# One decode step of attention and SwiGLU side by side: the products with V moved into the pass that scores the same group

## The chip, the core and the metric

The kernel runs on one core of one Trainium2 chip. Its time is the device time of one execution in microseconds; each figure is the median of several runs of the same program. The core has TensorE (PE in the profile, with PEld for its weight loads), VectorE (DVE), ScalarE (ACT), GpSimd (POOL) and SyncE (SP), and sixteen DMA engines that all queues share.

## What is computed

One token of four sequences goes through a layer norm, and then through two branches whose results are added to the input: attention over the last 4096 positions of a cache, and a SwiGLU feed-forward block.

```python
# B = 4 sequences, 1 token each, D = 512; Hq = 32 query heads, Hkv = 8, Dh = 128, W = 4096, F = 1792
xn = layernorm(x)
q = xn @ wq                                   # 32 heads of 128
k, v = k_cache[:, :, Sk - W:], v_cache[:, :, Sk - W:]     # each head of the cache serves 4 query heads
p = softmax(q k^T * Dh ** -0.5)
A = (p v).reshape(B, 1, Hq * Dh) @ wo
Bf = (silu(xn @ w_gate) * (xn @ w_up)) @ w_down
out = x + A + Bf
```

All inputs are bf16. What is read comes to 81 MB: 32 MiB each of K and V, 4 MiB each of wq and wo, and 1.75 MiB each of the three feed-forward matrices.

## The kernel before, in words

**Tiling.** The cache is worked off by head ("group"), eight of them. Position and sequence lie across the 128 partitions: a partition holds 128 consecutive positions of one sequence, so that a group's K is a tile of 128 partitions x 128 positions x 128 values (`KB`, 4 MiB), and V the same (`VB`). The scores of all 16 pairs of sequence and query head are computed for every position, and those of other sequences are masked out by a large negative shift. TensorE transposes K in chunks of eight positions (16 chunks, `transposes`, line 424) into three PSUM banks `ps_kt`; DVE (line 341) or, for five of the chunks, ACT (line 293) copies each to SBUF as `KT`; `scores` (line 437) multiplies it by the queries into one of four PSUM banks `ps_S`, 32 positions each. DVE takes maxima bank by bank (line 345). When all are there, `maxima` (line 444) transposes them, DVE forms the correction `CM` (lines 350 to 354), and `shift` (line 449) adds it to the four banks. ACT exponentiates each bank into `P` (line 297).

**Lag.** The products with V are one group behind. In pass r TensorE scores K of group r and, behind the shift, multiplies P of group r - 1 by V of group r - 1 (`pv`, line 460, 128 matmuls of 32 rows each, four column groups); pass 0 does this with zeros, for which POOL clears P and `VB` (lines 241 and 242). ACT's exponentials of pass r wait until `pv` of the same pass has read the old P (line 294, semaphore s_pv). The denominators are eight matmuls with ones ahead of `pv` (`dens`, line 468). DVE's `norm` (lines 356 to 368) sums the denominators (line 358), copies the product out of PSUM (line 360), waits for TensorE's `fin` (lines 476 and 477), which adds up the four parts, and writes the normalised result to `OT`. The spins (line 481) are matmuls whose result nobody reads.

**The order of the work** is written out by hand on each engine; nothing is scheduled. On TensorE a pass is: 16 chunks of transposes and scores, spins, `maxima`, spins, `shift`, `dens`, `pv`, three spins, `fin`. On DVE: copies and maxima, correction, and then `norm` of the previous group. The loop runs eight times. Behind it, outside the loop, stand `pv` and `dens` of the last group (lines 523 and 524), W_down (`down`, line 499), `fin` and `norm` of the last group, a permutation (line 531), and the products with W_o (lines 535 to 546): the first 22 of its 32 row tiles in one PSUM bank with four row groups, which ACT copies out (line 305), the other ten straight into the result, as the pieces of W_o land.

**Transfers.** SP's queue issues all the large ones, in one order (lines 261 to 275): wq, w_gate, w_up, K0 in two halves, then (when the projection is done, s_q) V7 into the buffer that held wq (`VL`), six row tiles of W_o, and then for each g from 1 to 7 the two halves of K(g) and V(g - 1); at the end W_down and the rest of W_o in four pieces. There is one buffer for K and one for V. A half of K is issued when the transposes of that half of the previous group are done (line 251), V when `pv` has read the V before (line 255). A wait on SP holds up everything that stands behind it.

Of the kernel before, what the change touches and what calls it, by code (L numbers as in the profile page):

```python
# [3 lines left out]
BF16 = mybir.dt.bfloat16  # L4
FP32 = mybir.dt.float32
# [5 lines left out]
def bass_parallel_sum__sliding_block_cached__swiglu_ffn__decode_kernel(  # L11
# [34 lines left out]
    OFF = -1.0e9  # L46
    WOS = (0, 6, 22, 27, 30, 32)
    WOE = 22
# [66 lines left out]
    O_ps = ps_O[:, 0:Dh]  # L115
    OL_ps = ps_kt[0][:, 0:Dh]
# [20 lines left out]
    d_out = sem("d_out")  # L137
    d_wo = [sem("d_wo%d" % q) for q in range(5)]
    d_k = [sem("d_k%d" % s) for s in range(2)]
    d_v = sem("d_v")  # L140
    d_vl = sem("d_vl")
    s_const = sem("s_const")
# [19 lines left out]
    s_pv = sem("s_pv")  # L162
    s_dp = sem("s_dp")
    s_oc = sem("s_oc")
    s_dn = sem("s_dn")
# [21 lines left out]
    with nc.Block() as block:  # L187

        @block.gpsimd
        def _(eng):  # L190
# [50 lines left out]
            eng.memset(P[:], 0.0)  # L241
            eng.memset(VB[:].rearrange("p t d -> p (t d)").bitcast(FP32), 0.0)  # L242
            eng.drain().then_inc(s_zero, 1)

        @block.sync
        def _(eng):
            H = NT // 2

            def load_k(g, h):
                if g > 0:  # L250
                    eng.wait_ge(s_tr, NCH * (g - 1) + (h + 1) * NCH // 2)
                eng.dma_start(KB[:, h * H:(h + 1) * H, :], kv_ap(A_k_cache, g, h * H, (h + 1) * H)).then_inc(d_k[h], 16)

            def load_v(g):
                eng.wait_ge(s_pv, g + 1)
                eng.dma_start(VB[:], kv_ap(A_v_cache, g, 0, NT)).then_inc(d_v, 16)  # L256
# [4 lines left out]
            eng.dma_start(WQ, wq_ap).then_inc(d_wq, 16)  # L261
# [12 lines left out]
            for q in range(1, 5):  # L274
                load_wo(q, WOS[q], WOS[q + 1])
            eng.wait_ge(s_y, 1)
            for n in range(2):
                eng.dma_start(out_ap[n], y[32 * n:32 * n + B, :]).then_inc(d_out, 16)
            eng.wait_ge(d_out, 64)

        @block.scalar
        def _(eng):
            eng.dma_start(X[:], x_ap).then_inc(d_x, 16)
            eng.wait_ge(s_var, 1)
            eng.activation(st_std[:], st_var[:], ACT.Sqrt).then_inc(s_std, 1)
            eng.wait_ge(s_const, 1)
            for n in range(4):
                eng.dma_start(X4[32 * n:32 * n + B, :], x4_ap[n]).then_inc(d_x4, 16)

            def group(r):  # L290
                for n, c in enumerate(ACT_CH):
                    eng.wait_ge(s_tr, r * NCH + (c + 1))
                    eng.activation(KT[:, c % 4], kt_ps[c % 3], ACT.Copy).then_inc(s_ea, 1)  # L293
                eng.wait_ge(s_pv, r + 1)
                for q in range(NB):
                    eng.wait_ge(s_mk, r * NB + (q + 1))
                    eng.activation(P[:, BT * q:BT * (q + 1), :], ps_S[q][:].rearrange("p (t n) -> p t n", n=NH),  # L297
                                   ACT.Exp, scale=SCALE).then_inc(s_p, 1)
# [12 lines left out]
        def _(eng):  # L311
# [24 lines left out]

            def group(r):
                for c in range(NCH):
                    if c not in ACT_CH:
                        eng.wait_ge(s_tr, r * NCH + (c + 1))  # L340
                        eng.tensor_copy(KT[:, c % 4], kt_ps[c % 3]).then_inc(s_ev, 1)  # L341
# [13 lines left out]

            def norm(r, O=O_ps):
                eng.wait_ge(s_dp, r + 2)
                eng.tensor_reduce(dsum[:], den_ps.rearrange("p (t n) -> p n t", n=NH), AX.X, ALU.add).then_inc(s_dn, 1)  # L358
                eng.wait_ge(s_pv, r + 2)
                eng.tensor_copy(Osb[:], O).then_inc(s_oc, 1)  # L360
                eng.wait_ge(s_fin, r + 2)
# [28 lines left out]
        def _(eng):  # L390
# [23 lines left out]
            eng.sem_inc(s_p, NB)  # L414
            eng.sem_inc(s_nrm, 2)
            eng.sem_inc(s_dn, 1)
            eng.sem_inc(s_oc, 1)
            eng.sem_inc(d_v, 16)

# [32 lines left out]

            def pv(r, V, O):
                for t in range(NT):
                    n = t % 4
                    if t % BT == 0:
                        eng.wait_ge(s_p, r * NB + (t // BT + 1))
                    if t % BT == BT - 1 and t < NT - 1:
                        eng.wait_ge(s_p, r * NB + (t // BT + 2))
                    last = mm(O[32 * n:32 * n + 32, :], P[:, t:t + 2, :].rearrange("p t n -> p (t n)"), V[:, t, :],  # L460
                              start=(t < 4), stop=(t >= NT - 4), skip_group_check=True)
                return last

            def dens(r):
                eng.wait_ge(s_p, r * NB + NB)
                for e in range(NT // DT):
                    n = e % 4
                    last = mm(den_ps[32 * n:32 * n + 32, :], ones[:, 0:32],  # L468
                              P[:, DT * e:DT * (e + 1), :].rearrange("p t n -> p (t n)"),
                              start=(e < 4), stop=(e >= NT // DT - 4), skip_group_check=True)  # L470
                return last

            def fin(r):
                eng.wait_ge(s_oc, r + 1)
                eng.wait_ge(s_dn, r + 1)
# [49 lines left out]
            down()  # L525
            eng.wait_ge(s_nrm, HKV + 1)
            fin(HKV)
            spin(2)
            eng.wait_ge(s_nrm, HKV + 2)
            for b in range(B):  # L530
# [3 lines left out]
            eng.wait_ge(s_pc, 1)  # L534
            for q in range(5):
                eng.wait_ge(d_wo[q], 16)
# [5 lines left out]
                if WOS[q + 1] == WOE:  # L542
                    last.then_inc(s_e, 1)
                if q == 2:
                    eng.wait_ge(s_ec, 1)
# [30 lines left out]
```

## Time and profile before

| | before |
|---|---|
| median of 3 runs | 198.21 us (197.14 to 198.66) |
| the profiled execution | 198.13 us |
| its span | 196.4 us |
| TensorE busy | 161.6 us (82% of the span) |
| DVE busy | 108.1 us (55%) |
| ACT busy | 61.0 us (31%) |
| POOL busy | 18.7 us (10%) |
| mean granted clock of TensorE | 0.972 |
| rate of the transfers over the span | 413 GB/s |

The span is the stretch that the profile covers; the 1.7 us around it are not in any row. A row of the timeline starts with its start and its length in microseconds, then engine, line, operation, output and inputs, and how many instructions it merges; in brackets stands how long the engine was idle before and what ended the idleness. The row of a window gives its stretch and length, then busy time and instructions of PE, PEld, DVE, ACT and POOL, the granted clock, the busy share of the DMA engines and GB/s. A row of transfers gives tile and source, queue, count, size of one, and the time from issue to landing; a landing is counted when all sixteen engines have delivered.

### The profile page before, as it was taken

What the parts mean: (1) busy time and instruction counts of PE and PEld (TensorE: products, weight loads), DVE (VectorE), ACT (ScalarE), POOL (GpSimd) and SP (SyncE); (2) the same over time, 40 slices, a digit from 0 to 9 for tenths busy, and PEclk for the clock granted to TensorE, in tenths of its full rate; (3) what the DMA queues carried; (4) which work ended last, traced back from release to release, by engine and by line L of the source; (5) the groups of instructions that cost most, each with busy time, mean ns of one, the idle gap of its engine ahead of it and who ended that gap; (6) DMA issues with size and microseconds to landing.
All of it is one profiled execution on the core that took longest, in us unless ns stands there. A gap on an engine that the chain in (4) does not pass through costs nothing.

```text
span 196.4 us, 8531 instructions
## 1 busy us (share of the span) xinstructions
PE 161.6 (82%) x3778; PEld 134.8 (69%) x3778; DVE 108.1 (55%) x217; ACT 61.0 (31%) x77; POOL 18.7 (10%) x52
## 2 busy tenths in 40 slices
PE   0137679938999979988998899799979999999983
PEld 0137679925996679568956895599459966994841
DVE  4205336841487268726872686268625882786240
ACT  2020004600562245233513451445042622550401
POOL 8879300000000000000000000000000000000000
PEclk9999999975999999999999999999996999999999
DMA  6999999989999999999999999999999999999991
GB/s 214 427 441 418 435 430 467 450 380 420 400 420 399 427 467 430 400 437 450 434 410 430 454 427 417 430 461 434 407 430 464 434 400 430 464 434 398 429 384 38
DMA packets 4833, 81.15 MB, mean 413 GB/s; under 512 B 596, under 2 KB 600, under 8 KB 1112
## 3 DMA queue, kind: packets, MB, share of 16 engines
q1 hardware_dynamic: 4768, 81.01, 96.8%
q8 instruction: 7, 0.11, 0.2%
q10 hardware_dynamic: 56, 0.01, 0.0%
q14 instruction: 2, 0.02, 0.0%
HBM read 81.01 MB, written 0.00 MB: 413 GB/s over the span
## 4 chain that ended last, share of the span: by engine, by line
DMA 63%; PE 30%; DVE 2%; SPq 2%; issue 2%; DVEq 0%
DMA kbuf<-in_A_k_cache_dram 50%; PE ps_kt L424 18%; DMA wo_sb<-in_A_wo_dram 13%; PE ps_s L437 5%; PE ps_o L460 2%; PE ps_kt L481 2%; PE ps_s L449 1%; DVE kT L341 1%; SPq L259 1%; PE ps_kt L468 0%; DVE mx L345 0%; SPq L273 0%; SPq L256 0%; PE ps_kt L444 0%; SPq L263 0%
## 5 line engine op out<-in xcount | busy, mean ns | idle before, releaser
L424 PE MATMUL ps_kt<-ident,kbuf 128*128 128x128 bf16 x1024 | 78.3, 224 | 8.7 <-DMA kbuf<-in_A_k_cache_dram 8.6
L341 DVE COPY kT<-ps_kt 128x1024 bf16<-128x1024 bf16 x88 | 57.8, 686 | 24.6 <-PE ps_kt L424 24.6
L424 PEld LDWEIGHTS ps_kt<-ident,kbuf 128*128 128x128 bf16 x1024 | 60.8, 100 | 9.4 <-DMA kbuf<-in_A_k_cache_dram 9.4
L293 ACT ACTIVATE kT<-ps_kt 128x1024 bf16<-128x1024 bf16 x40 | 40.9, 1023 | 41.3 <-PE ps_kt L424 41.3
L437 PE MATMUL ps_s<-qC,kT 128*128 128x16 bf16 x1024 | 44.9, 170 | 4.7 <-DVE kT L341 2.4
L437 PEld LDWEIGHTS ps_s<-qC,kT 128*128 128x128 bf16 x1024 | 37.2, 97 | 6.6 <-DVE kT L341 4.6
L297 ACT ACTIVATE p<-ps_s 128x512 bf16<-128x512 f32 x32 | 16.5, 603 | 60.6 <-PE ps_o L460 60.6
L345 DVE TENSOR_REDUCE mx<-ps_s 128x16 f32<-128x512 f32 x32 | 22.0, 689 | 5.9 <-PE ps_s L437 3.6
L481 PE MATMUL ps_kt<-own,ones 128*128 128x512 bf16 x98 | 25.2, 380 | 0.0
L460 PE MATMUL ps_o<-vbuf,p 128*32 128x128 bf16 x1024 | 16.6, 225 | 0.0
L460 PEld LDWEIGHTS ps_o<-vbuf,p 128*32 128x32 bf16 x1024 | 16.0, 101 | 0.1
L481 PEld LDWEIGHTS ps_kt<-own,ones 128*128 128x128 bf16 x98 | 7.7, 98 | 7.2
L449 PE MATMUL ps_s<-cm,own 128*128 128x512 bf16 x32 | 9.1, 412 | 1.0 <-DVE cm L354 1.0
L358 DVE TENSOR_REDUCE dsum<-ps_kt 128x16 f32<-128x256 f32 x8 | 3.4, 425 | 11.6 <-PE ps_kt L468 11.6
L395 PE MATMUL ps_s<-i,xn 4*128 4x4 f32 x4 | 0.6, 261 | 9.1 <-POOLq L232 9.1
L360 DVE COPY osb<-ps_o 128x128 f32<-128x128 f32 x7 | 2.0, 292 | 9.5 <-PE ps_o L460 9.5
L242 POOL MEMSET vbuf<- 128x8192 f32 x1 | 6.9, 6925 | 0.0
L395 PEld LDWEIGHTS ps_s<-i,xn 4*128 4x128 f32 x4 | 0.6, 208 | 9.1 <-POOLq L232 9.1
L449 PEld LDWEIGHTS ps_s<-cm,own 128*128 128x128 bf16 x32 | 2.6, 101 | 5.7 <-DVE cm L354 3.5
L402 PE MATMUL ps_s<-xnT,vlast 128*128 128x4 bf16 x128 | 3.6, 166 | 3.5 <-DMA vlast<-in_A_wq_dram 3.5
L402 PEld LDWEIGHTS ps_s<-xnT,vlast 128*128 128x128 bf16 x128 | 3.5, 104 | 3.6 <-issue 3.6
L362 DVE RECIPROCAL den<-ps_o 128x16 f32<-128x16 f32 x8 | 2.1, 258 | 6.4 <-PE ps_o L477 6.4
(88 smaller groups left out, 84.2 us busy)
## 6 DMA issues: line engine op xcount, KB each, us to landing
kbuf<-in_A_k_cache_dram SPq DMA_DIRECT2D x16, 2048.0 KB, 14.2
vbuf<-in_A_v_cache_dram SPq DMA_DIRECT2D x7, 4096.0 KB, 17.1
vlast<-in_A_wq_dram SPq DMA_DIRECT2D x1, 4096.0 KB, 12.3
vlast<-in_A_v_cache_dram SPq DMA_DIRECT2D x1, 4096.0 KB, 25.7
wo_sb<-in_A_wo_dram SPq DMA_DIRECT2D x1, 2048.0 KB, 23.6
wg_sb<-in_B_w_gate_dram SPq DMA_DIRECT2D x1, 1792.0 KB, 16.6
wu_sb<-in_B_w_up_dram SPq DMA_DIRECT2D x1, 1792.0 KB, 21.2
wd_sb<-in_B_w_down_dram SPq DMA_DIRECT2D x1, 1792.0 KB, 19.4
```

Of the source, the lines that this page charges most:

```text
L242: eng.memset(VB[:].rearrange("p t d -> p (t d)").bitcast(FP32), 0.0)
L293: eng.activation(KT[:, c % 4], kt_ps[c % 3], ACT.Copy).then_inc(s_ea, 1)
L297: eng.activation(P[:, BT * q:BT * (q + 1), :], ps_S[q][:].rearrange("p (t n) -> p t n", n=NH), ACT.Exp, scale=SCALE).then_inc(s_p, 1)
L341: eng.tensor_copy(KT[:, c % 4], kt_ps[c % 3]).then_inc(s_ev, 1)
L345: eng.tensor_reduce(mx[:, q, :], ps_S[q][:].rearrange("p (t n) -> p n t", n=NH), AX.X, ALU.max)
L358: eng.tensor_reduce(dsum[:], den_ps.rearrange("p (t n) -> p n t", n=NH), AX.X, ALU.add).then_inc(s_dn, 1)
L402: last = mm(q_ps[:, h * B:(h + 1) * B], WQ[:, c, h * Dh:(h + 1) * Dh], XnT[:, c, :], start=(c == 0 and h == 0), stop=(c == NC - 1), skip_g ...
L424: last = eng.transpose(kt_ps[c % 3][:, k, :], KB[:, CH * c + k, :], ident[:])
L437: last = mm(ps_S[q][:, NH * t:NH * (t + 1)], KT[:, c % 4, k, :], QC[:], start=(t == 0), stop=False, skip_group_check=True)
L449: mm(ps_S[q][:].rearrange("p (t n) -> p t n", n=NH), own[:], CM[:].unsqueeze(1).to_broadcast([128, BT, NH]), start=False, stop=True, skip_ ...
L460: last = mm(O[32 * n:32 * n + 32, :], P[:, t:t + 2, :].rearrange("p t n -> p (t n)"), V[:, t, :], start=(t < 4), stop=(t >= NT - 4), skip_ ...
L481: mm(ps_kt[k][:], ones[:], own[:].unsqueeze(1).to_broadcast([128, 4, 128]), skip_group_check=True)
```

## The change

- `pv` of pass r now takes P and V of group r. ACT's wait for s_pv goes; `pv` waits for each bank's exponentials of its own pass. The eight denominator matmuls stand between the PV matmuls, two for each bank of P, and write to another part of the PSUM bank that holds the product.
- The `pv`, `dens` and PSUM region behind the loop go. `fin` of the group before moves from the end of a pass to behind the third chunk's transposes; the first part of `norm` (copy of the product, sum of the denominators) stays at the end of DVE's pass, and the rest follows the copy of the third chunk in the next pass. Three spins at the end of a pass become four, and none in pass 0.
- SP issues K(g), V(g) for each g, W_down behind the first V, and all of W_o at the end, in four pieces of which the first has 22 row tiles. V(g) waits for `pv` of group g - 1. The wait for s_q goes, and wq has a buffer of its own.
- POOL no longer clears `VB`. TensorE waits for s_zero and for guT (the gated product) ahead of the loop.

```diff
-    WOS = (0, 6, 22, 27, 30, 32)
+    WOS = (0, 22, 27, 30, 32)
-    VL = sb("vlast", [128, NT, Dh], BF16, 512)
-    WQ = VL[:].rearrange("p t d -> p (t d)").rearrange("p (c n) -> p c n", c=NC)
+    WQ = sb("wq_sb", [128, NC, HQ * Dh], BF16, 512)
-    den_ps = ps_kt[1][:, 256:512]
+    den_ps = ps_O[:, 256:512]
...
@@ POOL
-            eng.memset(VB[:].rearrange("p t d -> p (t d)").bitcast(FP32), 0.0)
@@ SP
             def load_v(g):
-                eng.wait_ge(s_pv, g + 1)
+                if g > 0:
+                    eng.wait_ge(s_pv, g)
...
-            load_k(0, 0)
-            load_k(0, 1)
-            eng.wait_ge(s_q, 1)
-            eng.dma_start(VL[:], kv_ap(A_v_cache, HKV - 1, 0, NT)).then_inc(d_vl, 16)
-            load_wo(0, WOS[0], WOS[1])
-            for g in range(1, HKV):
+            for g in range(HKV):
                 load_k(g, 0)
                 load_k(g, 1)
-                load_v(g - 1)
-            eng.dma_start(WD[:], wd_ap).then_inc(d_wd, 16)
-            for q in range(1, 5):
+                load_v(g)
+                if g == 0:
+                    eng.dma_start(WD[:], wd_ap).then_inc(d_wd, 16)
+            for q in range(4):
                 load_wo(q, WOS[q], WOS[q + 1])
@@ ACT
-                eng.wait_ge(s_pv, r + 1)
                 for q in range(NB):
                     eng.wait_ge(s_mk, r * NB + (q + 1))
@@ DVE
+                    if c == 2 and rest:
+                        rest()
...
+                eng.wait_ge(s_pv, r + 1)
+                eng.tensor_copy(Osb[:], O_ps)
+                eng.tensor_reduce(dsum[:], den_ps.rearrange("p (t n) -> p n t", n=NH), AX.X, ALU.add).then_inc(s_dn, 1)
...
-                group(r)
-                norm(r - 1)
-            norm(HKV - 1, OL_ps)
+                group(r, lambda: norm(r - 1))
+            norm(HKV - 1)
@@ TensorE
+            eng.wait_ge(s_zero, 1)
+            eng.wait_ge(s_guT, 1)
...
-            def pv(r, V, O):
+            def pv(r):
                 for t in range(NT):
                     n = t % 4
                     if t % BT == 0:
-                        eng.wait_ge(s_p, r * NB + (t // BT + 1))
+                        eng.wait_ge(s_p, r * NB + (NB + t // BT + 1))
                     if t % BT == BT - 1 and t < NT - 1:
-                        eng.wait_ge(s_p, r * NB + (t // BT + 2))
+                        eng.wait_ge(s_p, r * NB + (NB + t // BT + 2))
...
+                    if t % DT == DT - 1:
+                        e = t // DT
+                        n = e % 4
+                        last = mm(den_ps[32 * n:32 * n + 32, :], ones[:, 0:32],
+                                  P[:, DT * e:DT * (e + 1), :].rearrange("p t n -> p (t n)"),
+                                  start=False, stop=(e >= NT // DT - 4), skip_group_check=True)
+                last.then_inc(s_pv, 1)
...
                     transposes(r, c)
+                    if c == 2:
+                        fin(r)
                     if c >= 2:
                         scores(r, c - 2)
...
                 shift(r)
-                eng.wait_ge(s_zero, 1)
-                dens(r).then_inc(s_dp, 1)
                 eng.wait_ge(s_nrm, r + 1)
                 eng.wait_ge(d_v, r * 16 + 16)
-                pv(r, VB, O_ps).then_inc(s_pv, 1)
-                spin(3)
-                fin(r)
-
-            eng.wait_ge(d_vl, 16)
-            pv(HKV, VL, OL_ps).then_inc(s_pv, 1)
-            dens(HKV).then_inc(s_dp, 1)
+                pv(r)
+                with eng.If(r > 0):
+                    spin(4)
             down()
```

More of the change, by code (lines that the diff above doesn't have):

```diff
@@ L115, in bass_parallel_sum__sliding_block_cached__swiglu_ffn__decode_kernel @@
     O_ps = ps_O[:, 0:Dh]
-    OL_ps = ps_kt[0][:, 0:Dh]
     O2_ps = ps_O[:, 128:128 + NH]
     D2_ps = ps_O[:, 192:192 + NH]
-    den_ps = ps_kt[1][:, 256:512]
+    den_ps = ps_O[:, 256:512]
     DT = 256 // NH
@@ L137, in bass_parallel_sum__sliding_block_cached__swiglu_ffn__decode_kernel @@
     d_out = sem("d_out")
-    d_wo = [sem("d_wo%d" % q) for q in range(5)]
+    d_wo = [sem("d_wo%d" % q) for q in range(4)]
     d_k = [sem("d_k%d" % s) for s in range(2)]
     d_v = sem("d_v")
-    d_vl = sem("d_vl")
     s_const = sem("s_const")
@@ L162, in bass_parallel_sum__sliding_block_cached__swiglu_ffn__decode_kernel @@
     s_pv = sem("s_pv")
-    s_dp = sem("s_dp")
-    s_oc = sem("s_oc")
     s_dn = sem("s_dn")
@@ L335, in _, with group @@
             eng.tensor_copy(QC[:], QT[:, 0])
-            def group(r):
+            def group(r, rest=None):
                 for c in range(NCH):
@@ L354, in group, with norm @@
                 eng.scalar_tensor_tensor(CM[0:NH, :], neg[:], M[:, 0:1], coff[:], ALU.mult, ALU.add).then_inc(s_cm, 1)
-            def norm(r, O=O_ps):
-                eng.wait_ge(s_dp, r + 2)
+                eng.wait_ge(s_pv, r + 1)
+                eng.tensor_copy(Osb[:], O_ps)
                 eng.tensor_reduce(dsum[:], den_ps.rearrange("p (t n) -> p n t", n=NH), AX.X, ALU.add).then_inc(s_dn, 1)
-                eng.wait_ge(s_pv, r + 2)
-                eng.tensor_copy(Osb[:], O).then_inc(s_oc, 1)
+            def norm(r):
                 eng.wait_ge(s_fin, r + 2)
@@ L414, in _ @@
             eng.sem_inc(s_p, NB)
-            eng.sem_inc(s_nrm, 2)
+            eng.sem_inc(s_nrm, 1)
             eng.sem_inc(s_dn, 1)
-            eng.sem_inc(s_oc, 1)
-            eng.sem_inc(d_v, 16)
+            eng.wait_ge(s_zero, 1)
+            eng.wait_ge(s_guT, 1)
             def transposes(r, c):
@@ L456, in pv @@
                     if t % BT == 0:
-                        eng.wait_ge(s_p, r * NB + (t // BT + 1))
+                        eng.wait_ge(s_p, r * NB + (NB + t // BT + 1))
                     if t % BT == BT - 1 and t < NT - 1:
-                        eng.wait_ge(s_p, r * NB + (t // BT + 2))
[L460 to L471, printed above, removed]
+                        eng.wait_ge(s_p, r * NB + (NB + t // BT + 2))
+                    mm(O_ps[32 * n:32 * n + 32, :], P[:, t:t + 2, :].rearrange("p t n -> p (t n)"), VB[:, t, :],
+                       start=(t < 4), stop=(t >= NT - 4), skip_group_check=True)
+                    if t % DT == DT - 1:
[5 more added lines that the diff above has]
+                last.then_inc(s_pv, 1)
             def fin(r):
-                eng.wait_ge(s_oc, r + 1)
                 eng.wait_ge(s_dn, r + 1)
@@ L513, in _ @@
                 shift(r)
[L514 to L515 removed]
                 eng.wait_ge(s_nrm, r + 1)
                 eng.wait_ge(d_v, r * 16 + 16)
[L518 to L524 removed]
+                pv(r)
+                with eng.If(r > 0):
+                    spin(4)
             down()
[L526 removed]
             fin(HKV)
             spin(2)
[L529 removed]
+            eng.wait_ge(s_nrm, HKV + 1)
             for b in range(B):
@@ L534, in _ @@
             eng.wait_ge(s_pc, 1)
-            for q in range(5):
+            for q in range(4):
                 eng.wait_ge(d_wo[q], 16)
@@ L543, in _ @@
                     last.then_inc(s_e, 1)
-                if q == 2:
+                if q == 1:
                     eng.wait_ge(s_ec, 1)
```

2 lines of the change are left out of this document (1 added, 1 removed).

## The prediction

> **What bounds the kernel now.** I read the page's slices first, then its chain of work, then the transfers by issue, and last the timeline of one steady pass and of the tail. "S" below is the moment at which the first half of a pass's K lands, "Ka" and "Kb" the halves.
>
> ```profile
> PEclk9999999975999999999999999999996999999999
> DMA  6999999989999999999999999999999999999991
> ...
> HBM read 81.01 MB, written 0.00 MB: 413 GB/s over the span
> ...
> DMA 63%; PE 30%; DVE 2%; SPq 2%; issue 2%; DVEq 0%
> ```
>
> The sixteen DMA engines are full from the second slice to the last but one. The windows view gives the rate over one pass:
>
> ```profile
> 94.00:113.40 19.40, 17.56 (x422) 14.57 (x417) 12.15 (x26) 7.18 (x9) 0.00 (x0) 1.00 1.01 432
> ```
>
> One pass moves 8192 KB (8.39 MB), which at 432 GB/s is 19.4 us: a pass takes exactly its transfers, and TensorE is busy for 17.56 us of it (third column). The loop is bound by transfers; the same 81.01 MB are read after the change. What can move is (a) whether the queue ever empties, (b) whether a pass's compute outgrows 19.4 us, (c) what follows the last transfer.
>
> For (a), issues on SP's queue, the time from issue to landing, and two links of the chain:
>
> ```profile
> 34.34 7.51 SPq L252 DMA_DIRECT2D kbuf<-in_A_k_cache_dram  x2
> 49.98 0.53 SPq L256 DMA_DIRECT2D vbuf<-in_A_v_cache_dram  x1
> ...
> 106.05 0.54 SPq L256 DMA_DIRECT2D vbuf<-in_A_v_cache_dram  x1
> ```
>
> ```profile
> kbuf<-in_A_k_cache_dram SPq DMA_DIRECT2D x1, 2048.0 KB, 12.7
> ```
>
> ```profile
> vbuf<-in_A_v_cache_dram SPq DMA_DIRECT2D x1, 4096.0 KB, 14.9
> ```
>
> ```profile
> vbuf<-in_A_v_cache_dram SPq DMA_DIRECT2D x1, 4096.0 KB, 17.1
> ```
>
> ```profile
> 94.04 14.51 DMA kbuf<-in_A_k_cache_dram
> ...
> 168.27 25.30 DMA wo_sb<-in_A_wo_dram
> ```
>
> The 12.7 belongs to Kb of pass 1 (issued at 34.34 + 7.51 - 0.54 = 41.3, landed 54.0), 14.9 to the first V (landed 64.9), 17.1 to the V issued at 106.05 (landed 123.15). The steady Ka lands at 94.04 + 14.51 = 108.55, its Kb 2.10 MB later (4.85 us, 113.4). So a steady V is issued 7.35 us before the Kb ahead of it lands, and lands 9.75 us behind it: 4.19 MB at full rate. The first V had a lead of 4.0 us and landed 10.9 us behind: 1.15 us lost, the only stall after the start. A lead under about 4.0 + 1.15 = 5.15 us empties the queue. The last piece of W_o lands at 193.57.
>
> For (b), one steady pass:
>
> ```profile
> 89.19 1.51 PE L424 MATMUL ps_kt<-ident,kbuf 128*128 128x128 bf16 x24 [1.50 <-DMA kbuf<-in_A_k_cache_dram]
> ...
> 92.10 0.69 DVE L341 COPY kT<-ps_kt 128x1024 bf16<-128x1024 bf16 x1 [0.37 <-PE ps_kt L424]
> ...
> 95.41 0.69 DVE L341 COPY kT<-ps_kt 128x1024 bf16<-128x1024 bf16 x1 [0.59 <-PE ps_kt L424]
> ...
> 102.85 1.03 PE L449 MATMUL ps_s<-cm,own 128*128 128x512 bf16 x4
> ...
> 103.81 0.40 PE L468 MATMUL ps_kt<-p,ones 128*32 128x256 bf16 x8
> ...
> 104.04 1.96 PE L460 MATMUL ps_o<-vbuf,p 128*32 128x128 bf16 x128
> ...
> 105.93 0.82 PE L481 MATMUL ps_kt<-own,ones 128*128 128x512 bf16 x3
> ...
> 106.13 2.06 ACT L297 ACTIVATE p<-ps_s 128x512 bf16<-128x512 f32 x4 [7.11 <-PE ps_o L460]
> 106.40 0.38 PEld L476 LDWEIGHTS ps_o<-dsum,head 128*128 128x128 f32 x2
> ...
> 106.73 0.37 PE L477 MATMUL ps_o<-sel,osb 128*128 128x16 f32 x2
> 107.14 0.26 DVE L362 RECIPROCAL den<-ps_o 128x16 f32<-128x16 f32 x1 [0.80 <-PE ps_o L477]
> ...
> 107.83 0.23 DVE L367 TENSOR_TENSOR oT<-on,dq 128x64 f32 x1 [0.18 <-issue]
> 108.59 1.34 PEld L424 LDWEIGHTS ps_kt<-ident,kbuf 128*128 128x128 bf16 x24 [1.59 <-DMA kbuf<-in_A_k_cache_dram]
> ```
>
> Scores take S to S+13.66 (89.19 to 102.85), shift and PV another 3.15 (to 106.00), spins and fin end at S+17.9, and TensorE waits 1.5 us for K. The exponentials, held back until PV of the group before has read P, run in that wait.
>
> **The change, part by part.**
>
> *Transfer order.* Ahead of K1 stood V7 (4096 KB) and six rows of W_o (768); now V0 (4096) and W_down (1792). Every later K stands 1024 KB (1.05 MB, 2.43 us) further back. Equally, behind K7a were Kb 2048 + V6 4096 + W_down 1792 + 26 rows of W_o 3328 = 11264 KB; now 2048 + 4096 + 4096 = 10240 KB. The wait for the projection (s_q) on SP goes, and nothing is late for it: six transfers and W_down are queued at once.
>
> *Start.* TensorE also waits for guT, some 0.3 us after the old start; pass 0 has the extra fin of 0.6 us. The memset of the V buffer on POOL goes; only s_zero hangs on it, which no pass waits for that early, so it costs and gives nothing. Pass 0 ends its PV thus before:
>
> ```profile
> 44.87 1.89 PE L449 MATMUL ps_s<-cm,own 128*128 128x512 bf16 x4 [1.03 <-DVE cm L354]
> ...
> 47.09 2.83 PE L460 MATMUL ps_o<-vbuf,p 128*32 128x128 bf16 x128
> ```
>
> That is 49.92; after, 49.92 + 0.3 + 0.6 + 0.2 = 51.0, when the next V (V1) is issued. K1b lands at 54.0 + 2.43 = 56.4: lead 5.4 us instead of 4.0, beside the 5.15 needed. Of the 1.15 us lost, 0 to 1.15 come back; I take 0.6, since the lead clears the need only just.
>
> *fin moved behind the third transpose.* It stood under the wait for K (cover 1.5 us); at the head of a pass it delays everything behind: 106.40 to 107.10, of which 0.6 is TensorE's own. Shift starts at S+14.26.
>
> *norm moved into DVE's copies.* 107.14 to 108.06, 0.92 us. DVE idles 0.37 and 0.59 us in the first half of a pass, and TensorE behind fin gives the copies 0.6 us more. Bounds 0 and 0.92; I take 0. What is queued behind it is the copy of chunk 4, for which the scores wait.
>
> *Exponentials ahead of PV.* One takes 2.06 / 4 = 0.515 us; the first starts when a quarter of the shift (0.26) is done and ends before the shift (1.03) does; the last ends 2.4 us behind the shift's start, when PV is in its third bank (1.1 + 2 x 0.49 = 2.1). They stay beside TensorE's work: 0 to 0.5, I take 0.
>
> *Denominators between PV matmuls.* Eight before PV cost 0.40 together. Alone, each between others on the same rows, at most 8 x 0.278 = 2.2 us (mean of the group in the view of groups by line, 80 to 145 us):
>
> ```profile
> L468 PE MATMUL ps_kt<-p,ones 128*32 128x256 bf16 x32 | 1.6, 278 | 0.0
> ```
>
> Row and bound are far apart; each now overlaps PV matmuls on three other column groups, nearer to the first: 0.75. PV ends 3.5 us behind the shift's start, S+17.76.
>
> *Osb and dsum copies* (0.8 us on DVE) lie beside the spins. Four spins instead of three: 4 x 0.273 = 1.09. TensorE is done at S+18.85, 0.55 us before the next K: the pass stays at 19.4. V's lead is 19.4 + 4.85 - 17.76 = 6.5 us, still over 5.15. V(r) itself lands at S+14.6, and the first PV matmul wants it at S+15.3: hidden by 0.7.
>
> [...]
>
> *The tail before:*
>
> ```profile
> 166.81 1.51 PE L424 MATMUL ps_kt<-ident,kbuf 128*128 128x128 bf16 x24
> ...
> 180.81 1.04 PE L449 MATMUL ps_s<-cm,own 128*128 128x512 bf16 x4
> ...
> 185.00 1.97 PE L460 MATMUL ps_kt<-vlast,p 128*32 128x128 bf16 x128
> ...
> 187.01 1.03 PE L487 MATMUL ps_s<-wd_sb,guT 128*32 128x512 bf16 x14
> ...
> 190.57 1.47 PE L487 MATMUL ps_s<-wo_sb,oP 128*32 128x512 bf16 x22 [0.37 <-DVE oP L384]
> ...
> 193.61 0.28 PE L491 MATMUL ps_s<-wo_sb,oP 128*4 128x128 bf16 x8 [0.25 <-DMA wo_sb<-in_A_wo_dram]
> 193.94 0.29 DVE L387 TENSOR_TENSOR y_sb<-ps_s,x 128x128 bf16<-128x128 f32 x1 [3.43 <-PE ps_s L491]
> ```
>
> The last PV and its denominators (185.00 to 187.01, 2.0 us) go; against them stands K7's 2.43. Step by step: K7a lands at 166.8 + 2.43 - 0.6 = 168.6; shift 182.9; PV ends 186.4; spins 187.5; W_down to 188.5; from there to the first W_o matmul 190.57 - 188.04 = 2.53, so 191.0; from there to y 3.37 less the 0.3 waited for W_o, 194.1. The last W_o lands at 193.57 - 0.6 = 193.0 and is not awaited. y starts at 194.1 against 193.94: **+0.2 us**.
>
> The profiled execution took 198.13 us (span 196.4 and 1.73 around it; median of the runs 198.21, 0.08 above). Sum: 198.13 + 0.2 = **198.3 us**.
>
> **Rivals.**
>
> 1. *The pass outgrows its transfers (slower).* If the interleaved denominators cost their bound, PV ends at S+19.2 and TensorE at S+20.3, 0.9 us late in each of six passes before the last: 5.4, and 1.45 in the last pass itself: 205 us. An exposed norm alone does it too: S+19.8, 0.4 x 6 + 0.92 = 3.3, so 201.6. It decides from a pass of 19.4, 0.55 above my sum. Against it: DVE's idle rows.
>
> 2. *The tail is hidden and the stall goes (no slower).* If all 1.15 us come back and the compute is shorter by my choices, y waits for W_o: 193.57 - 1.15 + 0.37 = 192.8, 197.0 us. For it: the lead of 5.4. It cannot go further, as the bytes stay.
>
> 3. *The clock.* The pass after this wait ran cold:
>
> ```profile
> 147.46 2.37 PE L424 MATMUL ps_kt<-ident,kbuf 128*128 128x128 bf16 x24 [1.58 <-DMA kbuf<-in_A_k_cache_dram]
> ...
> 162.43 1.04 PE L449 MATMUL ps_s<-cm,own 128*128 128x512 bf16 x4
> ```
>
> ```profile
> 148.00:149.00 1.00, 1.00 (x13) 1.00 (x11) 0.69 (x1) 0.00 (x0) 0.00 (x0) 0.50 0.99 426
> ```
>
> The granted clock was 0.50 after 1.58 us of idleness, though not after 1.50 at 89.19. Up to its shift that pass took 14.97 us (147.46 to 162.43) against 13.66, 1.3 more; in K7's pass it is not hidden: 199.6. With 0.55 us of idleness I think it rarer than before. [...]
>
> **How the numbers follow.** About 1% (2 us) is what a measurement of this kernel can tell from no change. Forecast 0.52, rival 2 0.15, rival 3 0.10, rival 1 0.23. Rival 1 is mostly past 200.3: slower 0.20. Faster than 196.2 needs a gain of which no row shows the source: 0.05. Same: 0.75. The range goes from rival 2, 197.0, to the exposed norm, 201.6, leaving the dear half of rival 1 and some of rival 2 out; the forecast's own is 197.5 to 199.2.
>
> **What would show it.** Right: passes of 19.4 us with a busy share of 1.0 and a wait for K of about 0.5; the first exponential within the shift; shift 14.3 behind S, PV ended by S+17.8; K7a at 168.6; TensorE, not W_o, last before y. Wrong: transposes that no longer wait for K, or V landing over 10 us behind Kb. The forecast fails if PV's stretch exceeds 4 us or the copies of chunks 4 to 7 fall behind norm.

## The result, and the profile after

The changed kernel took 196.88 us (median of 20 runs, 196.51 to 198.72) against 197.94 us for the kernel before (median of 20 runs beside them, 196.78 to 198.76). The ratio is 0.9952, with an interval of 0.9933 to 0.9972: 1.06 us faster, 0.5%. That lies within the 1% that the prediction called no change, but below its range: 198.3 us was forecast, and 197.0 was its lower end. The profiled execution took 196.62 us (span 194.9) against 198.13 before (span 196.4).

The page of the changed kernel: the span, the granted clock and the DMA share in 40 slices, the traffic, and the engines' shares of the chain that ended last.

```profile
span 194.9 us, 8285 instructions
...
PEclk9999999985999999999999999999999999999999
DMA  6999999999999999999999999999999999999991
...
HBM read 81.01 MB, written 0.00 MB: 416 GB/s over the span
...
DMA 63%; PE 32%; DVE 2%; issue 1%; ACT 0%; SPq 0%; DVEq 0%
```

The bytes are the same and the mean rate is 3 GB/s higher (416 for 413), so it is the transfers that have closed up. The slices, 4.9 us each, are too coarse to show where; the issues and landings do. In the loop TensorE's granted clock drops in pass 0 alone in this execution (0.50 from 42.3 to 49.1 us by the trace's records). The cold pass that the profile of before had later is not here, but it set no time: look 2 of the kernel before, below, has one too (from 146.57 us) and is as fast as the changed kernel.

Issues on SP's queue (start, duration of the issuing, what):

```profile
35.13 6.25 SPq L245 DMA_DIRECT2D kbuf<-in_A_k_cache_dram  x2
49.81 0.53 SPq L250 DMA_DIRECT2D vbuf<-in_A_v_cache_dram  x1
...
166.29 2.02 SPq L253 DMA_DIRECT2D wo_sb<-in_A_wo_dram  x4
```

The time from issue to landing (last column) of three of them: Kb of pass 1, the V behind it, and the last piece of W_o:

```profile
kbuf<-in_A_k_cache_dram SPq DMA_DIRECT2D x1, 2048.0 KB, 15.4
```

```profile
vbuf<-in_A_v_cache_dram SPq DMA_DIRECT2D x1, 4096.0 KB, 16.1
```

```profile
wo_sb<-in_A_wo_dram SPq DMA_DIRECT2D x1, 256.0 KB, 24.2
```

Kb of pass 1 is issued at 35.13 + 6.25 - 0.54 = 40.84 and lands at 56.24. The V of pass 1 (V1) is issued at 49.81, 6.4 us ahead of that, and lands at 65.91, 9.67 us behind it: its 4.19 MB at 434 GB/s, nothing lost. (That is called full rate below; the windows view gives 433 for the pass from here on.) Before, the lead was 4.0 us and the V landed 10.9 us behind. The same stretch, from the landing of K1's first half to that of K2's, in the windows view (length, busy time of PE, PEld, DVE, ACT and POOL, granted clock, DMA share, GB/s), first of the kernel before and then of the changed one:

```profile
49.14:69.80 20.66, 19.21 (x479) 15.86 (x465) 12.16 (x25) 9.24 (x13) 0.00 (x0) 1.00 1.00 414
```

```profile
51.33:70.76 19.43, 17.97 (x415) 14.51 (x415) 11.79 (x25) 7.19 (x9) 0.00 (x0) 1.00 1.01 433
```

20.66 us have become 19.43, a pass like any other. The DMA share, a share of time in which the engines hold packets, reads 1.00 in the one and 1.01 in the other; the gap shows in the bytes per second, 414 against 433. The packet records of the traces show why: the V behind Kb is 128 packets of 32 KB that take 1.21 us each, but 19 of them took over 1.3 us (up to 2.6) in the profile of before, and 1 in that of the changed kernel. A slow packet counts as busy: with the 19 of them the share still reads 1.00. The reader should take the rate, not the share, when asking whether a queue ran dry.

The last pass and the tail of the changed kernel, from the timeline:

```profile
167.73 1.51 PE L414 MATMUL ps_kt<-ident,kbuf 128*128 128x128 bf16 x24 [1.07 <-DMA kbuf<-in_A_k_cache_dram]
...
171.00 0.68 DVE L330 COPY kT<-ps_kt 128x1024 bf16<-128x1024 bf16 x1
...
181.65 1.03 PE L439 MATMUL ps_s<-cm,own 128*128 128x512 bf16 x4
182.07 2.07 ACT L286 ACTIVATE p<-ps_s 128x512 bf16<-128x512 f32 x4 [4.24 <-PE ps_s L439]
...
184.77 0.27 PE L455 MATMUL ps_o<-p,ones 128*32 128x256 bf16 x1
...
185.94 1.04 PE L473 MATMUL ps_s<-wd_sb,guT 128*32 128x512 bf16 x14
...
189.51 1.47 PE L473 MATMUL ps_s<-wo_sb,oP 128*32 128x512 bf16 x22 [0.37 <-DVE oP L374]
...
191.89 0.49 PE L477 MATMUL ps_s<-wo_sb,oP 128*4 128x128 bf16 x20
192.44 0.29 DVE L377 TENSOR_TENSOR y_sb<-ps_s,x 128x128 bf16<-128x128 f32 x1 [2.98 <-PE ps_s L477]
```

No W_o matmul is shown waiting for a transfer here, and the chain that ended last runs from K7's landing through TensorE; but the last W_o lands at 166.29 + 2.02 - 0.44 + 24.2 = 192.1 (the last of the four issues takes 0.44), and y starts 0.37 us behind it, as it did before (193.57 and 193.94). The compute behind K7 and the transfers now end together; the last W_o and y both come 1.5 us earlier than in the profile of before, where y waited for W_o.

### The profile page after: what moved, and what is told of

The parts are those of the page before. It is cut to its first block, busy times and chain, and to the rows that moved or that the text cites. A ratio compares the mean times of both kernels' runs of the same rounds, so it can differ in the third digit from the quotient of the medians.

```text
span 194.9 us, 8285 instructions
## 1 busy us (share of the span) xinstructions
PE 160.3 (82%) x3646; PEld 131.6 (68%) x3646; DVE 101.7 (52%) x217; ACT 61.1 (31%) x77; POOL 12.0 (6%) x51
## 3 DMA queue, kind: packets, MB, share of 16 engines
q1 hardware_dynamic: 4624, 81.01, 97.2%
HBM read 81.01 MB, written 0.00 MB: 416 GB/s over the span
## 4 chain that ended last, share of the span: by engine, by line
DMA 63%; PE 32%; DVE 2%; issue 1%; ACT 0%; SPq 0%; DVEq 0%
DMA kbuf<-in_A_k_cache_dram 52%; PE ps_kt L414 18%; DMA wu_sb<-in_B_w_up_dram 11%; PE ps_s L427 5%; PE ps_o L399 2%; PE ps_kt L467 2%; PE ps_s L473 1%; PE ps_o L463 1%; PE ps_o L450 1%; PE ps_o L462 1%; DVE kT L330 1%; PE ps_s L439 0%; PE ps_s L477 0%; DVE oP L374 0%; ACT s L294 0%
## 5 line engine op out<-in xcount | busy, mean ns | idle before, releaser
L414 PE MATMUL ps_kt<-ident,kbuf 128*128 128x128 bf16 x1024 | 76.5, 221 | 10.2 <-DMA kbuf<-in_A_k_cache_dram 8.2
L414 PEld LDWEIGHTS ps_kt<-ident,kbuf 128*128 128x128 bf16 x1024 | 59.2, 98 | 13.4 <-DMA kbuf<-in_A_k_cache_dram 13.4
L283 ACT ACTIVATE kT<-ps_kt 128x1024 bf16<-128x1024 bf16 x40 | 41.0, 1024 | 65.5 <-PE ps_kt L414 65.5
L467 PE MATMUL ps_kt<-own,ones 128*128 128x512 bf16 x102 | 25.9, 380 | 0.0
L450 PEld LDWEIGHTS ps_o<-vbuf,p 128*32 128x32 bf16 x1024 | 17.8, 102 | 4.6 <-ACT p L286 4.6
L450 PE MATMUL ps_o<-vbuf,p 128*32 128x128 bf16 x1024 | 19.2, 228 | 0.3
L455 PE MATMUL ps_o<-p,ones 128*32 128x256 bf16 x64 | 17.0, 287 | 0.0
L455 PEld LDWEIGHTS ps_o<-p,ones 128*32 128x32 bf16 x64 | 6.5, 101 | 0.0
L392 PE MATMUL ps_s<-xnT,wq_sb 128*128 128x4 bf16 x128 | 3.6, 166 | 3.4 <-DMA wq_sb<-in_A_wq_dram 3.4
L392 PEld LDWEIGHTS ps_s<-xnT,wq_sb 128*128 128x128 bf16 x128 | 3.5, 104 | 3.5 <-issue 3.5
```

The source lines that it names most:

```text
L392: last = mm(q_ps[:, h * B:(h + 1) * B], WQ[:, c, h * Dh:(h + 1) * Dh], XnT[:, c, :], start=(c == 0 and h == 0), stop=(c == NC - 1), skip_g ...
L414: last = eng.transpose(kt_ps[c % 3][:, k, :], KB[:, CH * c + k, :], ident[:])
L450: mm(O_ps[32 * n:32 * n + 32, :], P[:, t:t + 2, :].rearrange("p t n -> p (t n)"), VB[:, t, :], start=(t < 4), stop=(t >= NT - 4), skip_gro ...
L455: last = mm(den_ps[32 * n:32 * n + 32, :], ones[:, 0:32], P[:, DT * e:DT * (e + 1), :].rearrange("p t n -> p (t n)"), start=False, stop=(e ...
L467: mm(ps_kt[k][:], ones[:], own[:].unsqueeze(1).to_broadcast([128, 4, 128]), skip_group_check=True)
```

## The experiments

Two theories. *Stall:* the time is the transfers' time; what the kernel before lost, and the change gave back, is the hole in the queue ahead of the first V of the loop. Whether there is a hole is told by how long V is issued before the landing of the Kb ahead of it (the lead), and by how far behind that Kb it lands. *Tail:* the time is set by the compute behind K7's landing, which the change shortened by a PV and its denominators; then what shortens it further gains, and what brings K7 earlier gains too.

The table has every profiled execution. "Behind" is from the landing of Kb of pass 1 to that of the V behind it; its bytes alone take 9.7 us at the 433 GB/s above. "K7" is the start of the last pass's first transposes. All in us.

| kernel | lead | behind | K7 | last W_o lands | y starts | time |
|---|---|---|---|---|---|---|
| before | 4.0 | 10.9 | 166.81 | 193.57 | 193.94 | 198.13 |
| before, look 1 | 3.5 | 10.4 | 166.42 | 193.16 | 193.55 | 197.82 |
| before, look 2 | 5.1 | 9.7 | 165.44 | 192.20 | 192.57 | 196.84 |
| changed | 6.4 | 9.7 | 167.73 | 192.1 | 192.44 | 196.62 |
| a: lag, 14 rows ahead | 6.1 | 9.7 | 167.92 | 192.3 | 194.19 | 198.38 |
| b: changed, old queue | 3.65 | 10.35 | 166.28 | 193.01 | 193.39 | 197.57 |
| c: changed, W_down last | 1.4 | 11.8 | 165.67 | 194.4 | 195.53 | 199.70 |
| d: changed, shorter tail | 5.1 | 10.0 | 168.20 | 192.47 | 192.85 | 197.02 |
| e: before, idle PV skipped | 12.4 | 9.7 | 165.44 | 192.19 | 192.57 | 196.76 |
| f: changed, again | 6.4 | 9.7 | 167.76 | 192.09 | 192.47 | 196.73 |

### a: the kernel before, with as many bytes ahead of K1 as the change has

```
-    WOS = (0, 6, 22, 27, 30, 32)
+    WOS = (0, 14, 22, 27, 30, 32)
```

The first W_o load takes 14 rows instead of 6, 1024 KB more, which then don't stand behind K7.

> The kernel before with one constant changed: 14 row tiles of W_o instead of 6 ahead of K1, so 1024 KB more, as in the changed kernel; lag and tail stay. Stall theory (the gain is the first V's stall, cured by more bytes ahead of K1): lead of the first V 6.4 us instead of 4.0, it lands 9.7 us behind K1b instead of 10.9, the last W_o lands at 192.2 instead of 193.6, K7a at 167.9; the longer compute tail of the lagged kernel then ends last, y at 194.7, about 198.9 us, ratio 1.004. Tail theory (the gain is the PV that no longer stands behind the loop): the stall is no term, the last W_o stays at 193.6, K7a at 169.2, y at 196.0, about 200.2 us, ratio 1.011.

Measured: 198.43 us (12 runs), ratio 1.0043 (1.0020 to 1.0066). The first V:

```profile
34.81 6.58 SPq L252 DMA_DIRECT2D kbuf<-in_A_k_cache_dram  x2
50.23 0.54 SPq L256 DMA_DIRECT2D vbuf<-in_A_v_cache_dram  x1
```

```profile
kbuf<-in_A_k_cache_dram SPq DMA_DIRECT2D x1, 2048.0 KB, 15.5
```

```profile
vbuf<-in_A_v_cache_dram SPq DMA_DIRECT2D x1, 4096.0 KB, 15.8
```

Kb of pass 1 lands at 56.35, the V at 66.03: no hole, with the lag in place. Yet the kernel is slower than before, and its end says why:

```profile
167.92 1.51 PE L424 MATMUL ps_kt<-ident,kbuf 128*128 128x128 bf16 x24 [1.52 <-DMA kbuf<-in_A_k_cache_dram]
...
194.19 0.29 DVE L387 TENSOR_TENSOR y_sb<-ps_s,x 128x128 bf16<-128x128 f32 x1 [2.94 <-PE ps_s L491]
```

K7 and the last W_o land as in the changed kernel (within 0.2 us), but from K7 to y this kernel computes 26.27 us and the changed one 24.71. So y stands 1.9 us behind W_o. Here the tail sets the end, and 1.6 us is what the removed lag takes off it. Each theory is right in its place. Closing the hole was worth 1.2 us to the transfers, and the lag's last PV kept it from showing.

### b: the changed kernel with the queue of before

W_down and six rows of W_o change places: the six rows go behind the first V, W_down and 26 rows to the end.

```
-    WOS = (0, 22, 27, 30, 32)
+    WOS = (0, 6, 22, 27, 30, 32)
...
                 if g == 0:
-                    eng.dma_start(WD[:], wd_ap).then_inc(d_wd, 16)
-            for q in range(4):
+                    load_wo(0, WOS[0], WOS[1])
+            eng.dma_start(WD[:], wd_ap).then_inc(d_wd, 16)
+            for q in range(1, 5):
...
```

> The changed kernel with the amounts of the old queue: 6 row tiles of W_o behind the first V, W_down and 26 row tiles at the end. Stall theory: K1b lands 2.4 us earlier, the lead of the second V is 4.0 us, it lands about 10.9 us behind K1b, the last W_o at 193.4, y at 193.75 waiting for it, 197.9 us, ratio 1.000: taking the lag out alone brings nothing. Tail theory: the gain stays or grows, 196.9 us or less, ratio 0.995 or less.

Measured: 197.86 us (12 runs), ratio 1.0006 (0.9977 to 1.0035). Without the lag and with the old queue nothing is gained. The hole is there: lead 3.65, V1 10.35 us behind. K7 comes 1.45 us earlier than in the changed kernel, which the tail theory would have paid out; instead y waits for W_o:

```profile
193.05 0.28 PE L478 MATMUL ps_s<-wo_sb,oP 128*4 128x128 bf16 x8 [0.30 <-DMA wo_sb<-in_A_wo_dram]
193.39 0.29 DVE L378 TENSOR_TENSOR y_sb<-ps_s,x 128x128 bf16<-128x128 f32 x1 [4.82 <-PE ps_s L478]
```

With a this makes a square: lag and old queue 1.000, lag and the new amounts 1.0043, no lag and old queue 1.0006, no lag and new queue 0.9952. Neither half of the change gains; together they do, because the one closes the hole and the other keeps the later K7 from ending last.

### c: the changed kernel with still less ahead of K1

```
                 load_v(g)
-                if g == 0:
-                    eng.dma_start(WD[:], wd_ap).then_inc(d_wd, 16)
+            eng.dma_start(WD[:], wd_ap).then_inc(d_wd, 16)
```

> The changed kernel with W_down behind the last V instead of behind the first. Stall theory: K1b lands 4.25 us earlier, at 52.0, the second V is issued at 49.8 with a lead of 2.2, the queue is empty for about 2.9 us, the last W_o lands at 195.0, 199.5 us, ratio 1.008. Tail theory: more transfers cover the compute behind the last K, 196.9 us or less, ratio 0.995 or less.

Measured: 200.00 us (6 runs), ratio 1.0118 (1.0081 to 1.0154). V1 is issued only 1.4 us ahead of Kb's landing:

```profile
37.07 5.85 SPq L245 DMA_DIRECT2D kbuf<-in_A_k_cache_dram  x2
50.66 0.53 SPq L250 DMA_DIRECT2D vbuf<-in_A_v_cache_dram  x1
```

```profile
kbuf<-in_A_k_cache_dram SPq DMA_DIRECT2D x1, 2048.0 KB, 9.7
```

```profile
vbuf<-in_A_v_cache_dram SPq DMA_DIRECT2D x1, 4096.0 KB, 13.2
```

It lands 11.8 us behind: 2.1 us lost. That is 0.9 us more than in the profile of before, and the kernel is 2.1 us slower, so the slowdown needs a second term, and the tail has it:

```profile
191.37 2.75 PE L472 MATMUL ps_s<-wo_sb,oP 128*32 128x512 bf16 x22 [3.69 <-DMA wo_sb<-in_A_wo_dram]
```

```profile
191.00:192.00 1.00, 0.63 (x8) 0.35 (x12) 0.00 (x0) 0.00 (x0) 0.00 (x0) 0.50 0.98 405
```

With W_down at the end as well, all of W_o comes late; TensorE idles 3.69 us for it, its granted clock is 0.50 from 191 to 194 us, and the 22 matmuls that take 1.47 us in the changed kernel take 2.75. y stands 1.2 us behind the last W_o (194.4) instead of 0.37. So the direction is the stall theory's, and the excess is this clock.

### d: the changed kernel with a shorter tail

```
-            down()
             fin(HKV)
-            spin(2)
+            down()
```

The last pass's normalization is put ahead of W_down's matmuls, which then fill the wait that two spins filled.

> The changed kernel with fin of the last group ahead of W_down and without the two spins behind it: the chain from the last PV to y is 1.0 us shorter. Stall theory (the transfers set the end): y waits for the last W_o at 192.1, at most 0.1 us less, 196.8 us, ratio 0.995. Tail theory (compute behind the last K sets the end): 1.0 us less, 195.9 us, ratio 0.990.

Measured: 196.78 us (12 runs), ratio 0.9960 (0.9937 to 0.9982), as the changed kernel. The compute no longer ends last:

```profile
192.52 0.28 PE L477 MATMUL ps_s<-wo_sb,oP 128*4 128x128 bf16 x8 [0.28 <-DMA wo_sb<-in_A_wo_dram]
192.85 0.29 DVE L377 TENSOR_TENSOR y_sb<-ps_s,x 128x128 bf16<-128x128 f32 x1 [4.09 <-PE ps_s L477]
```

A shorter chain gains 0.1 us at most, for W_o ends behind it. So compute alone does not set the changed kernel's end; the tail theory falls for it. (In this execution V1 lost 0.3 us, most of the 0.4 us by which the last W_o lands later than in the changed kernel's profile.)

### e: the kernel before, its lag kept, with pass 0's idle PV skipped

In the kernel before, pass 0 multiplies a zeroed V buffer, which it needs for nothing, and the V of the loop can be loaded into that buffer only when this is done. Here pass 0 leaves that PV and its denominators out, so that V0 can be issued at once.

```
-            eng.memset(VB[:].rearrange("p t d -> p (t d)").bitcast(FP32), 0.0)
...
+            eng.sem_inc(s_dp, 1)
+            eng.sem_inc(s_pv, 1)
...
+            eng.wait_ge(s_zero, 1)
...
                 shift(r)
-                eng.wait_ge(s_zero, 1)
-                dens(r).then_inc(s_dp, 1)
...
-                pv(r, VB, O_ps).then_inc(s_pv, 1)
-                spin(3)
+                with eng.If(r > 0):
+                    dens(r).then_inc(s_dp, 1)
...
+                    pv(r, VB, O_ps).then_inc(s_pv, 1)
+                    spin(3)
```

> The kernel before, lag and queue contents as they are, but pass 0 leaves out its PV, denominators and spins (they multiply zeros and nobody reads the result), so that the first V is issued right behind K1b, at about 42, and the memset of the V buffer falls away. Stall theory: its lead is over 10 us, it lands 9.7 us behind K1b, the last W_o lands at 192.2 instead of 193.6, K7a at 165.5, y waits for W_o at about 192.7: 196.9 us, ratio 0.995, the whole gain of the change with the lag in place. Rival (the gain is the lag's removal, or the bytes ahead of K1 as such): last W_o at 193.6, 198 us, ratio 1.000.

Measured: 196.82 us (12 runs), ratio 0.9943 (0.9921 to 0.9966): all of the changed kernel's gain, with the lag, the queue and the PV behind the loop as before.

```profile
34.40 7.12 SPq L251 DMA_DIRECT2D kbuf<-in_A_k_cache_dram  x2
41.57 0.60 SPq L255 DMA_DIRECT2D vbuf<-in_A_v_cache_dram  x1
```

```profile
vbuf<-in_A_v_cache_dram SPq DMA_DIRECT2D x1, 4096.0 KB, 22.0
kbuf<-in_A_k_cache_dram SPq DMA_DIRECT2D x1, 2048.0 KB, 12.9
```

V0 is issued right behind Kb (40.98, landed 53.88) and lands at 63.57, 9.7 us behind it. K7 starts at 165.44, the last W_o lands at 192.19, and y waits for it. This is the cleanest test of the cause: the bytes, their order and the tail are those of before, and one transfer can be issued earlier. What else went is pass 0's idle matmuls and a memset. That they freed TensorE sooner brought the next transfer, K2's first half, forward by 0.2 us only (issued at 55.49 for 55.71), and that one had a lead of over 8 us in both.

### f: the changed kernel again, beside e

> The changed kernel as it is, beside the one without pass 0's PV on the same chip. Stall theory: both alike, 196.9 us, ratio 0.995. Rival (the lag's removal is the gain): this one 1 us faster than the other.

Measured: 196.86 us (12 runs), ratio 0.9941 (0.9920 to 0.9962), V1 issued at 49.85, 6.4 us ahead of Kb's landing, and landed 9.7 us behind it. e and f can't be told apart.

### g and h: two more looks at the kernel before

The 20 runs of the kernel before spread over 2 us, from 196.78 to 198.76; those of e and f over 0.5. If the hole is the cause, single executions of before should differ by it.

> The kernel before as it is, one more look, since its runs lie in two clusters about 1.2 us apart. Stall theory: the execution's time follows how far the first V lands behind K1b: 9.7 us with about 197.2, 10.9 us with about 198.3. Rival (the clusters come from the tail): the first V lands 10.9 us behind in both.

> The same kernel, another look, with the same expectations: by the stall theory the time follows the landing of the first V behind K1b (9.7 us with 197.2, 10.9 us with 198.3); by the rival it does not.

Measured: 197.82 us with 10.4 us behind, and 196.84 us with 9.7 us behind. The second is as fast as the changed kernel, and it had no hole: its V0 was issued at 48.81, 5.1 us ahead of Kb's landing (53.92). In look 1 it was issued at 50.54, 1.73 later. Of these, 1.08 arise ahead of the shift. The timeline of look 1:

```profile
31.44 1.01 PE L424 MATMUL ps_kt<-ident,kbuf 128*128 128x128 bf16 x8
...
44.65 1.89 PE L449 MATMUL ps_s<-cm,own 128*128 128x512 bf16 x4 [1.03 <-DVE cm L354]
```

The same two steps in look 2:

```profile
31.12 0.61 PE L424 MATMUL ps_kt<-ident,kbuf 128*128 128x128 bf16 x8
...
43.57 1.89 PE L449 MATMUL ps_s<-cm,own 128*128 128x512 bf16 x4 [1.03 <-DVE cm L354]
```

Three groups of eight transposes at the start of pass 0 take about 1.0 us each in look 1 (30.38, 31.44 and 32.51), and 0.61 in look 2. The other 0.65 us arise behind the shift. The windows view, look 1 and then look 2:

```profile
48.00:50.00 2.00, 2.00 (x88) 2.00 (x80) 0.00 (x0) 0.00 (x0) 0.00 (x0) 0.50 0.99 426
```

```profile
48.00:50.00 2.00, 2.00 (x69) 1.63 (x57) 0.00 (x0) 1.10 (x3) 0.00 (x0) 1.00 1.05 451
```

In both the granted clock had fallen to 0.50 ahead of the shift; by the trace's records it was back at 47.6 us in look 2, and at 50.3 in look 1. The second part goes with the granted clock, whose moments differ between executions of one kernel. Of the first the traces show only where the slow groups end: in each look where the first record of the granted clock begins (33.3 us in look 1, 30.5 in look 2); which clock was granted ahead of it they do not show. So the kernel before lost 1.15, 0.7 and 0 us in the three executions profiled; the changed kernel with its longer lead (6.4, 6.4 and 5.1 us in the changed kernel, f and d) lost 0, 0 and 0.3.

## Why the prediction was wrong

**Bound and bytes: right.** The same 81.01 MB are read, and a steady pass takes 19.36 us (109.51 - 90.15) where 19.4 was forecast. The starts of two passes in the changed kernel's timeline:

```profile
90.15 1.51 PE L414 MATMUL ps_kt<-ident,kbuf 128*128 128x128 bf16 x24 [1.05 <-DMA kbuf<-in_A_k_cache_dram]
...
109.51 1.51 PE L414 MATMUL ps_kt<-ident,kbuf 128*128 128x128 bf16 x24 [1.07 <-DMA kbuf<-in_A_k_cache_dram]
```

**"K's stand 1024 KB (2.43 us) further back": right.** Kb of pass 1 landed at 56.24 against 54.0 before, 2.2 later, and in a, with the same bytes ahead, at 56.35.

**"Of the 1.15 us lost, 0 to 1.15 come back; I take 0.6": this step failed.** All came back (V landed 9.67 us behind Kb instead of 10.85). The lead was 6.4 us, not 5.4, because V1 was issued at 49.81 and not at 51.0. The forecast's own terms came as it said, or a little more: pass 0 started 0.42 us later (28.26 for 27.84), fin and what else lies ahead of the shift added some 0.7, PV with its denominators 0.3, together 1.4 for 1.1. What failed is the base to which they were added. Pass 0 in the execution profiled before had a gap of 1.66 us in the midst of its matmuls, for which the timeline names no releaser, and one slow group of transposes and part of a second. First the kernel before, then the changed one:

```profile
30.63 1.01 PE L424 MATMUL ps_kt<-ident,kbuf 128*128 128x128 bf16 x8
...
40.63 0.19 PE L437 MATMUL ps_s<-qC,kT 128*128 128x16 bf16 x2 [1.66 <-issue]
```

```profile
31.82 0.69 PE L414 MATMUL ps_kt<-ident,kbuf 128*128 128x128 bf16 x8
...
40.06 0.29 PE L427 MATMUL ps_s<-qC,kT 128*128 128x16 bf16 x6 [0.39 <-issue]
```

The gap is 1.27 us shorter and the slow groups cost 0.4 less; that is more than the terms added. How much of this is owed to the change the runs don't tell. The gap was 1.66, 1.06 and 1.00 us in three looks at the kernel before, 1.27 in e and 0.73 in a, and 0.39, 0.88 and 0.52 in the changed kernel, f and b, so without the lag it may be shorter. The slow groups vary with the execution: in d, with the same pass 0 as the changed kernel, they cost 1.8 us and V1 was issued at 51.25, even later than forecast. So the lead of 6.4 is in part luck.

The need of 5.15 us was about right: with a lead of 5.1, nothing was lost in look 2 and 0.3 us in d; with 3.5 and 3.65, 0.7 and 0.65; with 1.4, 2.1. It is no sharp line, and the lead alone does not set the loss, as 4.0 lost 1.15, more than 3.5 did. But then 5.4, forecast as clear of it, gives all or nearly all of the stall back. Taking half was a hedge between the ends and not a reading.

**The tail: right in its steps, too long in its sum.** Its sum is the second thing that failed, by the size of its terms. From K7's start to y 25.5 us were forecast and 24.7 measured. fin at the head of the pass was priced at 0.6 us and cost 0.26: the shift starts 13.92 us behind K7's start (181.65 - 167.73) against 13.66 before and 14.26 forecast. That the rest lies under a wait for DVE's copies is inferred from DVE's timeline, not tried. The rest is three small terms: PV with its denominators ends 3.39 us behind the shift's start (185.04 - 181.65) for 3.5, spins and W_down 0.15, and W_o to y 0.14 less than forecast.

**"norm costs 0" and "exponentials 0": right.** norm ran between two DVE copies, chunk 4's copy came at 171.00, at once behind it, and the pass kept its length; the exponentials start 0.42 us behind the shift's start and stay ahead of PV.

**"Denominators 0.75": right** (3.39 for 3.5, as above).

**"The last W_o lands at 193.0 and is not awaited; +0.2": the times were wrong** for these two reasons together. K7 started at 167.73, not 168.6 (0.55 more of the stall, some 0.3 less at the start), and the chain was 0.8 shorter: y at 192.44 for 194.1. The last W_o landed at 192.1 for 193.0. That it is not awaited held in the profiles of the changed kernel and of f, but by less than 0.05 us and not by the 0.7 us forecast (194.1 less 193.0 and the 0.37 from W_o to y).

**Rival 2 is what happened, nearly.** It said: all of the stall goes, y waits for W_o at 192.8, 197.0 us; the run gave 192.44 and 196.62 in the profile, with W_o and the compute ending together. It had the chance 0.15, because the forecast gave back half of the stall and charged fin in full. Rivals 1 and 3 didn't come: in the changed kernel's profile TensorE still waits 1.05 to 1.15 us for K ahead of passes 3 to 7, so a pass did not outgrow its transfers, and the clock stayed at 1.00 behind these waits. (The forecast had 0.55 us of waiting; the smaller cost of fin, PV and the spins is the difference.)

**Against which "before" the gain counts.** The forecast was made against one execution that had lost 1.15 us. Look 2 shows one without a loss. The change hardly lowers the floor (196.78 is the fastest of 20 runs of before, 196.51 of the changed kernel); it takes away most runs above it: 19 of its 20 lie at 197.3 or below, against 5 of 20 before.

**What stays open.** That an early issue of the first V takes the loss away is shown by a and e, and that a late one brings it by b and c; how large the loss is at a given lead is not explained. That pass 0 takes different times in different executions was seen (slow groups, the clock, the gap of 0.39 to 1.66 us), but none of these was varied on its own. The traces do show one thing beside the gap. In all ten of them a 16 KB packet of a queue that the DMA view calls "instruction" starts late in pass 0 (at 38.24 us in the profile of before, at 37.78 in that of the changed kernel). In the eight with a gap, the gap ends 2.2 to 2.4 us behind that start (at 40.63 and 40.06 in these two), whatever its length. In c and d TensorE came to this place later and was held up by 0.3 us or less. Whether TensorE waits for this packet no run shows.

## What to carry to other kernels

In a loop bound by transfers, look for a place where the queue runs dry, and read it from the rate between two landings and from each transfer's landing behind the one ahead; the busy share read 1.00 here all the same. Ask of a transfer that waits for a buffer how long it is issued before the landing of the one ahead: here the V behind Kb of pass 1 lost nothing with a lead of 6.1 us or more, 0 and 0.3 us with 5.1, and 0.65 to 2.1 with 4.0 or less. The short lead of the kernel before came about in the first pass of a pipelined loop, which had idle work and, in its profile, a granted clock of 0.50 for 6.8 us. If two ends (last transfer, last compute) lie within a microsecond, a change that moves one of them may gain nothing, as a and b did; e gained because it moved K7 and the last W_o together. Find out by a square of four kernels, and price each end at its own bound before taking a middle.

## What the runs showed of the hardware

- **A lead of about 5 us was needed to keep this queue full**, though the transfers ahead are large. By the table, the V behind Kb of pass 1 lost nothing with a lead of 6.1 to 12.4 us (a, changed, f, e), 0 and 0.3 us with 5.1 (look 2 and d), and 1.15, 0.65, 0.7 and 2.1 us with 4.0, 3.65, 3.5 and 1.4 (before, b, look 1 and c). With the lead of 1.4 us the 4096 KB took 13.2 us from issue to landing, 3.5 more than their 9.7 at full rate.
- **The parts of a transfer don't end together, and a V issued late starts with slow packets.** In the profile of before, ten of the sixteen 4-byte packets that close Kb of pass 1 had started by 52.05 us, 2.0 us ahead of its landing at 54.02, and of its sixteen completion signals the first came at 52.14, the tenth at 52.39 and the last at 54.02. The first packet of the V behind it started 1.98 us behind the issue (51.96 - 49.98). Of V's 128 packets, over 1.3 us instead of 1.21 took 19 in before, 14 in look 1, 13 in b and 17 in c; 4 in look 2 and 5 in d; and 1 each in the changed kernel, f, a and e.
- **TensorE's speed differs between executions of one kernel.** At the start of pass 0 groups of eight transposes took 1.0 us instead of 0.61: none in look 2, three in look 1, five in c. They end where the trace's first record of the granted clock begins (30.5, 33.3 and 37.2 us; 31.9 in before); ahead of it the windows view prints 1.00 because there is no record, so the durations are the witness there. After that the stretches at 0.50 inside the loop lasted 3.4 us (before, from 147.9), 6.8 (before, the changed kernel and both looks, in pass 0) or 10.2 (e, in pass 0).
- **Idleness of one length was followed by either clock.** In the profile of before TensorE idled 1.58 us for K ahead of 147.46, and the granted clock was 0.50 from 147.91 on; behind 1.57 us ahead of 128.04 it stayed at 1.00, and 24 transposes took 1.51 us there against 2.37. In c it was at 0.50 behind 3.69 us.
